# Turning the tail's first MLP layer around, and splitting the last output group

## The chip, the core and the metric

The kernel runs on one core of a Trainium2 chip. The metric is the time of one execution on the device in microseconds (us); the median of several runs is given. The profile is of one further execution, whose span from the first to the last instruction is 275.7 us.

## The reference

The computation is a linear attention followed by a gated MLP that mixes along the sequence.

```python
def phi(x):                               # x: (8, 8, 576, 64), w_phi: (64, 128)
    proj = np.einsum('bhsd,df->bhsf', x, w_phi)
    proj = proj - np.max(np.abs(proj), axis=-1, keepdims=True)
    return np.concatenate([np.exp(proj), np.exp(-proj)], axis=-1)
kv  = einsum('bhsf,bhsd->bhfd', phi(k), v);  z = phi(k).sum(2)
x   = einsum('bhsf,bhfd->bhsd', phi(q), kv) / (phi(q) @ z + 1e-6)   # -> (8, 576, 512)
h   = np.maximum(x @ w_in, 0)             # w_in: (512, 1024)
u, v = h[..., :512], h[..., 512:]
v_n = (v - mean(v)) / np.sqrt(var(v) + 1e-6)          # over the 512 features
v_s = einsum('ts,bsd->btd', w_spatial, v_n) + b_spatial[None, :, None]
out = (u * v_s) @ w_out                   # w_out: (512, 512)
```

The two halves u and v of the first MLP layer are what the change is about: v is normalized over its features and mixed over the tokens, u is multiplied with the result.

## The kernel before, in words

A batch has 576 tokens: four groups of 128 ("main") and 64 left over (the "tail", `TL = 64`). The tails of two successive batches share a tile, batch 2g in partitions 0 to 63 and batch 2g+1 in partitions 64 to 127; `bl` says which, and `r` is the slice of partitions or columns that belongs to it.

The attention (functions `a_...`) runs in units of a pair of heads, one after the other; in step i the stages of several units are interleaved by the list `ORDER`. When a batch's attention is done, `b_tasks(b)` puts the batch's MLP work in a queue, as (cost, function). After each stage of a step, `fill` takes tasks off the queue at a rate that spreads the queue's total cost over the steps that are left until the next batch's tasks come; the cost is an estimate of TensorE time, `MM` for four 512-column matmuls. So the matmuls of the MLP lie between those of the attention. What is left after the last step is issued in the queue's order. Within this the framework's scheduler may still order independent instructions of an engine differently.

The MLP of a batch, in the queue's order: an output group of the batch before; `b_v_tail` (the tail's v); two main groups of v (`b_v`); another output group; the other two of v; the roots and the tail's normalization (`b_root_tail`, `b_ln_tail`, `b_root`); normalization of the main v (`b_ln`) between output groups of the batch before and the four groups of u (`b_u`); `b_u_tail`; the mixing `b_s` and `b_s_tail`. The output of batch b waits for the queue of batch b + 1; that of the last batch stands at the end, the four main groups `b_o` and then `b_o_tail`.

Main v (`v_mm`, L447 to L451): for each 128 tokens, four matmuls with the tokens (xT) stationary and 512 columns of w_in moving, so the result has tokens in partitions; ACT applies the relu to a tile `vr` (L449); DVE takes mean and variance with bn_stats (L450) and bn_aggr (L451). `moments` (L455, L456) and `root` (on POOL, L461, L462) make scale and shift, and `normalize` (L467) writes `vn`, or `vnt` for the tail, on POOL and in the last batch on DVE. `b_v_tail` uses the same `v_mm` with the tail's 64 columns of `xTt` stationary.

Main u (`b_u`, L515, L517): w_in is stationary and the 512 tokens move, so the result has features in partitions, as `b_s` needs it. `b_u_tail` (L527, L529) does so for the 64 tokens of a tail: sixteen matmuls of 64 columns.

`b_s` (L536, L537, L539) needs all four `vn` tiles of its batch and `vnt`; DVE multiplies its result into `uT`. `b_s_tail` is L548 to L554. `o_mm` (L561, L564) makes an output group: four matmuls of 512 columns, a copy that alternates between DVE and ACT to a tile `ob`, and a transfer issued on SP's queue (L570 main, L576 tail, one for each batch of the pair).

[...] `vr` has five buffers, `ob` six, `uTt` one.

Of the kernel before, what the change touches and what calls it, by code (L numbers as in the profile page):

```python
# [8 lines left out]
FP32 = mybir.dt.float32  # L9
BF16 = mybir.dt.bfloat16  # L10
AF = mybir.ActivationFunctionType
# [5 lines left out]
def kernel(  # L17
# [15 lines left out]
    nc = tc.nc  # L33

    B, H, S, D = q.shape
    F = w_phi.shape[1]
    DM = moe_w_in.shape[0]
    DFF = moe_w_in.shape[1]
    HALF = DFF // 2
    P = 128  # L40
    KC = DM // P
    NP = H // 2
    NB = 4
    T0 = NB * P
    TL = S - T0
    G = B // 2
    POS = [0, 2, 1, 3]
    DA = D + 2

    cpool = ctx.enter_context(tc.tile_pool(name="const", bufs=1))  # L50
# [4 lines left out]
    s2 = ctx.enter_context(tc.tile_pool(name="stage_b", bufs=2))  # L55

    psum = ctx.enter_context(tc.tile_pool(name="psum", bufs=8, space=bass.MemoryType.PSUM))
# [13 lines left out]
    st = {}  # L71
    gs = {}
# [47 lines left out]
        pin(nc.sync.dma_start_transpose)(out=u[x + "T"], in_=src.rearrange("p h x -> p (h x)"))  # L120


    wphi_f = cpool.tile([P, F], FP32)
    for i in range(2):
        pin(nc.scalar.dma_start)(out=wphi_f[i * D:(i + 1) * D, :], in_=w_phi)
    alloc(0)
# [12 lines left out]
    bias = cpool.tile([P, NB], FP32)  # L139
# [4 lines left out]
    ident = cpool.tile([P, P], BF16)  # L144
# [40 lines left out]
    for y in range(2):  # L185
        r = slice(y * D, (y + 1) * D)
# [7 lines left out]
    for i in range(2):  # L194
        pin(nc.scalar.copy)(out=alternate(wm, i),
                            in_=wphi2[:, i * F:(i + 1) * F].unsqueeze(1).to_broadcast([P, NP, F]))
# [19 lines left out]
    w_in_bf = cpool.tile([P, KC, DFF], BF16)  # L216
    w_out_bf = cpool.tile([P, KC, DM], BF16)
# [226 lines left out]
    def v_mm(lhs, dst, r, stats, mv):  # L444
        pv = psum.tile([P, HALF], FP32, tag="bank", name="pv")
        for kc in range(KC):
            nc.tensor.matmul(out=pv[r], lhsT=lhs(kc), rhs=w_in_bf[:, kc, HALF:DFF],  # L447
                             start=(kc == 0), stop=(kc == KC - 1))
        nc.scalar.activation(out=dst[r], in_=pv[r], func=AF.Relu, bias=0.0, scale=1.0)  # L449
        nc.vector.bn_stats(out=stats[r], in_=dst[r])  # L450
        nc.vector.bn_aggr(out=mv[r], in_=stats[r])  # L451

    def moments(mv, r, n):
        m = small.tile([P, NB, 2], FP32, tag="var", name="var")
        nc.vector.tensor_scalar(out=m[r, 0:n, 0:1], in0=mv[r, 0:n, 1:2], scalar1=1e-6, scalar2=None, op0=ALU.add)  # L455
        nc.vector.tensor_scalar(out=m[r, 0:n, 1:2], in0=mv[r, 0:n, 0:1], scalar1=-1.0, scalar2=None, op0=ALU.mult)  # L456
        return m
# [11 lines left out]
    def b_v(b, j):  # L469
        d = st[b]  # L470
        if j == 0:
            d["vn"] = s2.tile([P, NB, HALF], BF16, tag="vn", name="vn", bufs=2)
            d["mv"] = small.tile([P, NB, 2], FP32, tag="mv", name="mv")
            d["vr"] = {}
        d["vr"][j] = s2.tile([P, HALF], BF16, tag="vr", name="vr", bufs=5)
        stats = small.tile([P, 6], FP32, tag="stats", name="stats")
        v_mm(lambda kc: d["xT"][:, kc, j * P:(j + 1) * P], d["vr"][j], slice(0, P), stats, d["mv"][:, j, :])
        if j == NB - 1:
            d["var"] = moments(d["mv"], slice(0, P), NB)

    def b_root(b):
        st[b]["rs"] = root(st[b]["var"], slice(0, P), NB)

    def b_ln(b, j):
        d = st[b]
        normalize(b, d["vn"][:, j, :], d["vr"][j], d["rs"][:, j, :])

    def b_v_tail(g, bls):
        d = gs[g]
        r = slice(bls[0] * TL, (bls[-1] + 1) * TL)  # L490
        vr = s2.tile([P, HALF], BF16, tag="vr", name="vr", bufs=5)
        stats = small.tile([P, 6], FP32, tag="stats", name="stats")
        mv = small.tile([P, 1, 2], FP32, tag="mv_t", name="mv_t")
        v_mm(lambda kc: d["xTt"][:, kc, r], vr, r, stats, mv[:, 0, :])
        d["ln"] = vr, moments(mv, r, 1)

    def b_root_tail(g, bls):
        d = gs[g]
        r = slice(bls[0] * TL, (bls[-1] + 1) * TL)
        d["rs"] = root(d["ln"][1], r, 1)  # L500

    def b_ln_tail(g, bls):
        d = gs[g]
        vr = d["ln"][0]
        for bl in bls:
            r = slice(bl * TL, (bl + 1) * TL)
            normalize(2 * g + bl, vnt[g % 2][r, bl, :], vr[r], d["rs"][r, 0, :])

    def b_u(b, dc):
        d = st[b]  # L510
        if dc == 0:
            d["uT"] = s2.tile([P, KC, T0], BF16, tag="uT", name="uT", bufs=1)
        pu = psum.tile([P, T0], FP32, tag="bank", name="pu")
        for kc in range(KC):
            nc.tensor.matmul(out=pu, lhsT=w_in_bf[:, kc, dc * P:(dc + 1) * P], rhs=d["xT"][:, kc, :],  # L515
                             start=(kc == 0), stop=(kc == KC - 1))
        nc.scalar.activation(out=d["uT"][:, dc, :], in_=pu, func=AF.Relu, bias=0.0, scale=1.0)  # L517

    def b_u_tail(g, bls):
        d = gs[g]  # L520
        if bls[0] == 0:
            d["uTt"] = s2.tile([P, KC, P], BF16, tag="uTt", name="uTt", bufs=1)
        r = slice(bls[0] * TL, (bls[-1] + 1) * TL)
        pu = psum.tile([P, KC, P], FP32, tag="bank", name="pu")
        for dc in range(KC):
            for kc in range(KC):
                nc.tensor.matmul(out=pu[:, dc, r], lhsT=w_in_bf[:, kc, dc * P:(dc + 1) * P],  # L527
                                 rhs=d["xTt"][:, kc, r], start=(kc == 0), stop=(kc == KC - 1))
        nc.scalar.activation(out=d["uTt"][:, :, r], in_=pu[:, :, r], func=AF.Relu, bias=0.0, scale=1.0)  # L529

    def b_s(b, dc):
        d = st[b]
        ps = psum.tile([P, T0], FP32, tag="bank", name="ps")
        cs = slice(dc * P, (dc + 1) * P)
        for sp in range(NB):
            nc.tensor.matmul(out=ps, lhsT=d["vn"][:, sp, cs], rhs=w_spT[:, sp, 0:T0], start=(sp == 0), stop=False)  # L536
        nc.tensor.matmul(out=ps, lhsT=vnt[b // 2 % 2][:, b % 2, cs], rhs=w_spT[:, NB + b % 2, 0:T0],  # L537
                         start=False, stop=True)
        nc.vector.tensor_tensor(out=d["uT"][:, dc, :], in0=ps, in1=d["uT"][:, dc, :], op=ALU.mult)  # L539
# [18 lines left out]
    def o_mm(lhs, r):  # L558
        po = psum.tile([P, DM], FP32, tag="bank", name="po")
        for dc in range(KC):  # L560
            nc.tensor.matmul(out=po[r], lhsT=lhs(dc), rhs=w_out_bf[:, dc, :], start=(dc == 0), stop=(dc == KC - 1))  # L561
        ob = s2.tile([P, DM], FP32, tag="ob", name="ob", bufs=6)
        turn[0] ^= 1
        (nc.vector.tensor_copy if turn[0] else nc.scalar.copy)(out=ob[r], in_=po[r])  # L564
        return ob

    def b_o(b, j):
        ob = o_mm(lambda dc: st[b]["uT"][:, dc, j * P:(j + 1) * P], slice(0, P))
        dst = bass.AP(tensor=out.tensor, offset=out.offset + b * S * DM + POS[j] * DM, ap=[[NB * DM, P], [1, DM]])
        nc.sync.dma_start(out=dst, in_=ob)  # L570

    def b_o_tail(g, bls):
        r = slice(bls[0] * TL, (bls[-1] + 1) * TL)
        ob = o_mm(lambda dc: gs[g]["uTt"][:, dc, r], r)
        for bl in bls:
            nc.sync.dma_start(out=out[2 * g + bl, T0:S, :], in_=ob[bl * TL:(bl + 1) * TL, :])  # L576
# [18 lines left out]
    MM = KC * T0 / 2400.0  # L595
    MS = (KC + 1) * T0 / 2400.0

    def out_tasks(b):
        ts = [(MM, lambda j=j: b_o(b, j)) for j in range(NB)]
        if b % 2:  # L600
            ts.append((MM, lambda: b_o_tail(b // 2, [0, 1])))
        return ts

    def b_tasks(b):

        g, bl = b // 2, b % 2
        outs = out_tasks(b - 1) if b else []
        vs = [(MM, lambda j=j: b_v(b, j)) for j in range(NB)]
        us = [(MM, lambda dc=dc: b_u(b, dc)) for dc in range(KC)]
        ss = [(MS, lambda dc=dc: b_s(b, dc)) for dc in range(KC)]  # L610
        ns = [(0.0, lambda j=j: b_ln(b, j)) for j in range(NB)]
        ts = outs[:1] + [(MM, lambda: b_v_tail(g, [bl]))] + vs[:2] + outs[1:2] + vs[2:]
        ts += [(0.0, lambda: b_root_tail(g, [bl])), (0.0, lambda: b_ln_tail(g, [bl])), (0.0, lambda: b_root(b))]
        if b == 0:
            ts += [(0.3, lambda i=i: transpose_spatial(i)) for i in range(NB + 2)]
        for y in range(NB):
            ts += ns[y:y + 1] + outs[2 + y:3 + y] + us[y:y + 1]
        ts += [(MM / 2, lambda: b_u_tail(g, [bl]))] + ss
        ts.append((MS / 2, lambda: b_s_tail(g, [bl])))
        return ts + (out_tasks(b) if b == B - 1 else [])  # L620

# [147 lines left out]
```

## Time and profile before

| | |
|---|---|
| time, median of 3 runs | 279.08 us (278.86 to 280.59) |
| profiled span | 275.7 us, TensorE clock 1.00 throughout |
| TensorE (PE) busy | 254.7 us, 92% |
| VectorE (DVE) busy | 236.5 us, 86% |
| ScalarE (ACT) busy | 218.1 us, 79% |
| GpSimd (POOL) busy | 184.4 us, 67% |
| chain that ended last | PE 70%, ACT 14%, DVE 11%, issue 3% |

PE is the matmul stream and PEld the weight loads that run beside it. "Busy" adds up the time in which an engine has an instruction in it; matmuls are pipelined, so a 512-column matmul lasts 379 ns while the next starts 216 ns later. In the groups' rows, the number after x is how often the group ran; then come its busy time and the mean of one in ns, then the idle time of the engine just before it and what ended that. In the waits, the three numbers are the total in us, the count and the longest. In the chain, a row is the start, the time by which the piece moved the end on, and what it was. In the timeline, a row is the start, the time taken, engine, line and operation, and in brackets the idle time before.

### The profile page before, as it was taken

To read this page: it belongs to the slowest core of one execution; us is meant where nothing else is said; L and a number is where in the kernel's file an instruction comes from. 1 tells how busy PE (TensorE), PEld (TensorE's weight loads), DVE (VectorE), ACT (ScalarE), POOL (GpSimd) and SP (SyncE) were. 2 spreads that over 40 slices of the span, in tenths; PEclk is the share of its full clock that TensorE was granted. 3 is DMA by queue.
4 is the path that set the end of the run, shared out by engine and by line. 5 is a ranking of instruction groups with operands and counts; after the bars stand their busy time and mean duration, and the time that the engine had idled before them with its cause. 6 is when DMAs were issued, how large, how long until landed. Compare 5 with 4: busy or idle time off the path is not lost.

```text
span 275.7 us, 8138 instructions
## 1 busy us (share of the span) xinstructions
PE 254.7 (92%) x3007; PEld 171.3 (62%) x3047; DVE 236.5 (86%) x614; ACT 218.1 (79%) x501; POOL 184.4 (67%) x312
## 2 busy tenths in 40 slices
PE   3778999999999999999998999999998999999993
PEld 2467776777665766666665775766655765554441
DVE  7989999879999889998889899988898897565751
ACT  7898999797698978999798979998798977633511
POOL 7999899999569945897787954997347632410200
PEclk9999999999999999999999999999999999999999
DMA  7999999999999997999999998899744301211115
GB/s 209 230 228 146 164 155 113 181 208 122 202 200 219 232 212 133 232 176 199 156 110 221 258 183 146 171 233 176 104 89 118 88 2 73 81 40 40 76 40 190
DMA packets 84840, 42.43 MB, mean 154 GB/s; under 512 B 51840, under 2 KB 80192, under 8 KB 84800
## 3 DMA queue, kind: packets, MB, share of 16 engines
q1 hardware_dynamic: 60240, 30.95, 54.5%
q0 software_dynamic: 24400, 10.89, 38.5%
q8 instruction: 24, 0.39, 0.6%
q14 instruction: 16, 0.13, 0.2%
q10 hardware_dynamic: 160, 0.07, 0.1%
HBM read 32.85 MB, written 9.44 MB: 153 GB/s over the span
## 4 chain that ended last, share of the span: by engine, by line
PE 70%; ACT 14%; DVE 11%; issue 3%; ACTq 0%; DVEq 0%
PE pv L447 10%; PE ps L536 10%; PE po L561 9%; PE pu L515 8%; PE ps L266 7%; ACT kf L281 7%; PE pv L378 4%; PE pn L398 4%; ACT qf L365 4%; DVE mk L278 3%; PE pq L344 3%; PE ps L537 2%; PE pn L426 2%; ACT vr L449 1%; PE pu L527 1%
## 5 line engine op out<-in xcount | busy, mean ns | idle before, releaser
L306 POOL TENSOR_TENSOR vs<-v_f,em 128x512 bf16<-128x512 f32 x64 | 65.4, 1042 | 27.8 <-ACT em L301 25.3
L281 ACT ACTIVATE kf<-ps 128x512 bf16<-128x512 f32 x144 | 75.4, 638 | 6.5 <-DVE mk L278 6.5
L365 ACT ACTIVATE qf<-pq 128x512 bf16<-128x512 f32 x128 | 66.6, 625 | 9.6 <-PE pq L344 7.5
L278 DVE TENSOR_REDUCE mk<-ps 128x4 f32<-128x512 f32 x72 | 46.3, 681 | 0.7
L292 DVE TENSOR_REDUCE mq<-ps 128x4 f32<-128x512 f32 x62 | 39.9, 678 | 2.2 <-PE ps L266 2.0
L561 PE MATMUL po<-w_out_bf,uT 128*128 128x512 bf16 x120 | 31.9, 379 | 1.4 <-ACT kf L281 0.8
L461 POOL TENSOR_TENSOR rs<-var,neghalf 64x1 f32<-64x1 f32 (+1 forms) x16 | 12.8, 797 | 30.5 <-DVE var L456 30.3
L536 PE MATMUL ps<-w_spT,vn 128*128 128x512 bf16 x119 | 32.5, 379 | 0.5
L450 DVE BATCH_NORM_STATS2 stats<-vr 128x6 f32<-128x512 bf16 (+1 forms) x40 | 26.7, 684 | 6.5 <-ACT vr L449 6.2
L447 PE MATMUL pv<-w_in_bf,xT 128*128 128x512 bf16 x117 | 30.7, 379 | 1.2 <-ACT kf L281 0.6
L515 PE MATMUL pu<-xT,w_in_bf 128*128 128x512 bf16 x119 | 31.1, 379 | 0.5 <-issue 0.2
L449 ACT ACTIVATE vr<-pv 128x512 bf16<-128x512 f32 (+1 forms) x40 | 23.8, 620 | 8.9 <-PE pv L447 8.1
L539 DVE TENSOR_TENSOR uT<-ps,uT 128x512 bf16<-128x512 f32 x32 | 22.0, 687 | 8.5 <-PE ps L537 7.6
L378 PE MATMUL pv<-vs,kf 128*128 128x66 bf16 x512 | 24.5, 193 | 1.3 <-ACT kf L281 1.1
L389 DVE TENSOR_TENSOR x<-pn,rc 128x256 bf16<-128x256 f32 x64 | 25.0, 416 | 0.3
L398 PEld LDWEIGHTS <-qf 128*128 128x128 bf16 x512 | 20.2, 97 | 7.4 <-issue 1.7
L517 ACT ACTIVATE uT<-pu 128x512 bf16<-128x512 f32 x32 | 19.7, 643 | 6.3 <-PE pu L515 3.2
L378 PEld LDWEIGHTS <-kf 128*128 128x128 bf16 x512 | 21.7, 97 | 3.6 <-issue 2.9
L398 PE MATMUL pn<-kv,qf 128*128 128x66 bf16 x512 | 21.9, 193 | 0.9 <-ACT kf L281 0.3
L380 PE MATMUL pv<-vst,kf 128*128 128x66 bf16 x128 | 21.2, 192 | 1.4 <-POOL vst L61 1.4
L564 ACT COPY ob<-po 128x512 f32<-128x512 f32 x18 | 11.0, 613 | 14.3 <-PE po L561 8.8
L467 POOL TENSOR_SCALAR vn<-vr,rs 128x512 bf16<-128x512 bf16 x28 | 21.2, 764 | 0.9
(130 smaller groups left out, 562.6 us busy)
## 6 DMA issues: line engine op xcount, KB each, us to landing
out_dram<-ob SPq DMA_DIRECT2D x32, 256.0 KB, 2.7
v_f<-in_v_dram SPq DMA_DIRECT2D x14, 512.0 KB, 5.6
k_bf<-in_k_dram POOLq DMA_DIRECT2D x14, 256.0 KB, 6.3
q_bf<-in_q_dram POOLq DMA_DIRECT2D x14, 256.0 KB, 5.9
qt<-qT_b SPq DMA_DIRECT2D x24, 64.0 KB, 4.2
v_tl<-in_v_dram SPq DMA_DIRECT2D x8, 128.0 KB, 5.9
v_f<-in_v_dram SPq DMA_DIRECT2D x1, 1024.0 KB, 8.8
w_in_bf<-in_moe_w_in_dram POOLq DMA_DIRECT2D x2, 512.0 KB, 7.0
```

Source lines behind the costliest of these rows:

```text
L278: nc.vector.tensor_reduce(out=u["mk"][:, hs], in_=pk, axis=AX.X, op=ALU.max, apply_absolute_value=True)
L281: nc.scalar.activation(out=u["kf"][:, s, hs, :], in_=pk, func=AF.Exp, bias=0.0, scale=sc)
L292: nc.vector.tensor_reduce(out=mq[:, 4 * half:4 * half + 4], in_=pq, axis=AX.X, op=ALU.max, apply_absolute_value=True)
L306: nc.gpsimd.tensor_tensor(out=vs[:, s, :, 0:D], in0=st[u["b"]]["v"][:, pj * H:(pj + 1) * H, :], in1=em[:, s, :].unsqueeze(2).to_broadcast( ...
L365: nc.scalar.activation(out=qf[:, s], in_=pq, func=AF.Exp, bias=0.0, scale=sc)
L378: nc.tensor.matmul(out=pv[:, hh, s, :], lhsT=u["kf"][:, s, 4 * hh + c, :], rhs=u["vs"][:, s, 4 * hh + c, :], start=(c == 0), stop=False)
L398: nc.tensor.matmul(out=pn[:, pos, :], lhsT=u["qf"][hh][:, s, pos, :], rhs=d["kv"][:, 2 * u["pj"] + hh, s, :], start=(s == 0), stop=(s == 1))
L447: nc.tensor.matmul(out=pv[r], lhsT=lhs(kc), rhs=w_in_bf[:, kc, HALF:DFF], start=(kc == 0), stop=(kc == KC - 1))
L450: nc.vector.bn_stats(out=stats[r], in_=dst[r])
L515: nc.tensor.matmul(out=pu, lhsT=w_in_bf[:, kc, dc * P:(dc + 1) * P], rhs=d["xT"][:, kc, :], start=(kc == 0), stop=(kc == KC - 1))
L536: nc.tensor.matmul(out=ps, lhsT=d["vn"][:, sp, cs], rhs=w_spT[:, sp, 0:T0], start=(sp == 0), stop=False)
L561: nc.tensor.matmul(out=po[r], lhsT=lhs(dc), rhs=w_out_bf[:, dc, :], start=(dc == 0), stop=(dc == KC - 1))
```

## The change

The tail's first MLP layer is done for u and v at once with w_in stationary: 32 matmuls of 64 moving columns into one PSUM bank, and two relus to `uTt` and `vTt`, both with features in partitions. v is needed with tokens in partitions, so a new task `b_turn_tail`, placed after the first two main groups of v, turns `vTt` back by four transposes on TensorE; DVE copies the result to `vr` and takes its statistics. `b_u_tail` goes away. `vTt` takes a buffer of `vr`'s ring, and `uTt` gets a second buffer, as it's now written earlier; the room comes from `wphi_f`, which moves from the constants to the ring of `ob`.

In the last batch the output order becomes: first main group, tail, the two middle groups, last main group. This last one (`b_o_last`) is made in two halves of 256 columns, each with its own PSUM bank; the first is copied by ACT and sent on ACT's queue, the second copied by DVE and sent on SP's. It is for shortening the time after the last matmul.

```diff
-    wphi_f = cpool.tile([P, F], FP32)
+    wphi_f = s2.tile([P, F], FP32, tag="ob", name="wphi_f", bufs=6)
...
     def b_v_tail(g, bls):
         d = gs[g]
+        if bls[0] == 0:
+            d["uTt"] = s2.tile([P, KC, P], BF16, tag="uTt", name="uTt", bufs=2)
+        d["vTt"] = s2.tile([P, KC, TL], BF16, tag="vr", name="vTt", bufs=5)
         r = slice(bls[0] * TL, (bls[-1] + 1) * TL)
+        pu = psum.tile([P, 2 * KC, TL], FP32, tag="bank", name="pu")
+        for dc in range(2 * KC):
+            for kc in range(KC):
+                nc.tensor.matmul(out=pu[:, dc, :], lhsT=w_in_bf[:, kc, dc * P:(dc + 1) * P],
+                                 rhs=d["xTt"][:, kc, r], start=(kc == 0), stop=(kc == KC - 1))
+        nc.scalar.activation(out=d["vTt"], in_=pu[:, KC:2 * KC, :], func=AF.Relu, bias=0.0, scale=1.0)
+        nc.scalar.activation(out=d["uTt"][:, :, r], in_=pu[:, 0:KC, :], func=AF.Relu, bias=0.0, scale=1.0)
+
+    def b_turn_tail(g, bls):
+        d = gs[g]
+        r = slice(bls[0] * TL, (bls[-1] + 1) * TL)
+        pt = psum.tile([P, KC, P], BF16, tag="bank", name="pt")
+        for dc in range(KC):
+            nc.tensor.transpose(out=pt[r, dc, :], in_=d["vTt"][:, dc, :], identity=ident)
         vr = s2.tile([P, HALF], BF16, tag="vr", name="vr", bufs=5)
...
-        v_mm(lambda kc: d["xTt"][:, kc, r], vr, r, stats, mv[:, 0, :])
+        nc.vector.tensor_copy(out=vr[r], in_=pt[r].rearrange("p n e -> p (n e)"))
+        nc.vector.bn_stats(out=stats[r], in_=vr[r])
+        nc.vector.bn_aggr(out=mv[r, 0, :], in_=stats[r])
         d["ln"] = vr, moments(mv, r, 1)
...
-    def b_u_tail(g, bls):
...
+    def b_o_last(b, j):
+        dst = bass.AP(tensor=out.tensor, offset=out.offset + b * S * DM + POS[j] * DM, ap=[[NB * DM, P], [1, DM]])
+        for y, copy, queue_ in ((0, nc.scalar.copy, nc.scalar), (1, nc.vector.tensor_copy, nc.sync)):
+            n = slice(y * DM // 2, (y + 1) * DM // 2)
+            po = psum.tile([P, DM // 2], FP32, tag="bank", name="po")
+            for dc in range(KC):
+                nc.tensor.matmul(out=po, lhsT=st[b]["uT"][:, dc, j * P:(j + 1) * P], rhs=w_out_bf[:, dc, n],
+                                 start=(dc == 0), stop=(dc == KC - 1))
+            ob = s2.tile([P, DM], FP32, tag="ob", name="ob", bufs=6)
+            copy(out=ob[:, 0:DM // 2], in_=po)
+            queue_.dma_start(out=dst[:, n], in_=ob[:, 0:DM // 2])
...
+        if b == B - 1:
+            ts = ts[:1] + ts[-1:] + ts[1:NB - 1] + [(MM, lambda: b_o_last(b, NB - 1))]
...
-        ts = outs[:1] + [(MM, lambda: b_v_tail(g, [bl]))] + vs[:2] + outs[1:2] + vs[2:]
+        ts = outs[:1] + [(MM, lambda: b_v_tail(g, [bl]))] + vs[:2]
+        ts += [(MM / 4, lambda: b_turn_tail(g, [bl]))] + outs[1:2] + vs[2:]
...
-        ts += [(MM / 2, lambda: b_u_tail(g, [bl]))] + ss
+        ts += ss
```

More of the change, by code (lines that the diff above doesn't have):

```diff
@@ L517, in b_u @@
         nc.scalar.activation(out=d["uT"][:, dc, :], in_=pu, func=AF.Relu, bias=0.0, scale=1.0)
-    def b_u_tail(g, bls):
[L520 to L529, printed above, removed]
     def b_s(b, dc):
```

## The prediction

> **What bounds the kernel now.** I read the page's first part (busy time of each engine), then the table of stretches, then the chain that ended last in order of time.
>
> ```profile
> PE 254.7 (92%) x3007; PEld 171.3 (62%) x3047; DVE 236.5 (86%) x614; ACT 218.1 (79%) x501; POOL 184.4 (67%) x312
> ```
> ```profile
> 100.00:140.00 40.00, 39.58 (x474) 26.74 (x480) 37.09 (x92) 35.64 (x84) 29.14 (x52) 1.00 1.07 175
> 140.00:180.00 40.00, 38.84 (x475) 26.36 (x480) 37.54 (x99) 35.73 (x85) 29.50 (x50) 1.00 1.18 186
> ```
>
> The columns of the stretches are the length, then PE, weight loads, DVE, ACT and POOL. PE is busy 39.6 of 40 us, and a busy PE need not be a full one; the chain is the better witness, where each entry's length is what it advanced the end:
>
> ```profile
> 110.63 1.03 PE pv L447 x4
> ...
> 126.79 0.47 PE pu L527 x16
> ```
> ```profile
> 244.28 0.22 PE pt L412 x4
> ```
>
> Elsewhere in that chain four 512-column matmuls advance PE by 0.86 us (0.216 each), sixteen 64-column ones (L527) by 0.47 (0.029 each) and four transposes by 0.22 (0.055 each). Between about 40 and 271 us the chain is mostly such runs: PE's issue rate sets the time. It leaves PE for ACT and DVE only around 76-91, 105-110, 145-150 and 199-210 us, at the start of a batch's MLP work. The waits of PE that these cost are short:
>
> ```profile
> PE pv L378 <- ACT kf L281: 1.1, 1, 1.1
> PE pt L259 <- ACT kf L281: 1.0, 1, 1.0
> ...
> PE po L561 <- ACT kf L281: 0.8, 1, 0.8
> ```
>
> DVE is second: 37.1 to 37.5 of 40 us, only 2.5 to 2.9 us free per 40.
>
> [...] a 128x512 bf16 copy out of PSUM takes 413 ns (L261), the fp32 one 678 (L564). [...] On SP's queue here, the last issues landed after 2.2 to 2.4 us.
>
> **The change part by part.** The rows I price it with:
>
> ```profile
> L449 ACT ACTIVATE vr<-pv 64x512 bf16<-64x512 f32 x8 | 4.7, 593 | 3.6 <-PE pv L447 3.6
> L529 ACT ACTIVATE uTt<-pu 128x256 bf16<-128x256 f32 x8 | 3.7, 469 | 0.0
> L261 DVE COPY qt<-pt 128x512 bf16<-128x512 bf16 x12 | 5.0, 413 | 0.3 <-PE pt L259 0.3
> ```
>
> *PE, per tail.* Removed: four matmuls of 512 columns, 0.86, and the sixteen of b_u_tail, 0.47; together 1.33 us. Added: 32 matmuls of 64 columns, 32 x 0.0294 = 0.94, and four transposes with 128 moving columns, 0.22; together 1.16. Net -0.17 us. There are eight tails. In the seven before the last batch PE sets the time, so 7 x -0.17 = **-1.2 us**.
>
> *ACT, per tail.* One 593 ns relu and one 469 ns relu become two of 469 ns: 1.06 to 0.94, -0.12 us in all. But they now both stand ahead of the batch's first b_v relus: 0.94 in place of 0.59 there, +0.35 us where the chain already visits ACT. The later u slot gives 0.47 back. I take zero, as PE's waits on ACT are few.
>
> *DVE, per tail.* One copy of a 64x512 bf16 bank, by L261 0.41 us (row length, not rows, sets it: the 64- and the 128-row bn_stats take 688 and 683). It replaces nothing, so 7 x 0.41 = 2.9 us lie on the second-busiest engine. Low end 0 (it fits in the free time), high end 2.9 (PE waits for all of it). I take **+0.3 us**: the waits list only short waits of PE on DVE after the start.
>
> *The new wait.* PE's transposes wait for the vTt relu. Two b_v groups (8 x 0.216 = 1.7 us of PE) stand between; the two relus need 0.94. Hidden unless ACT is over 1 us behind; behind the transposes on PE stand o1 and the later b_v groups. Buffers: vTt and vr together make six allocations per batch in a ring of five, but each reuses a tile of an earlier stage that has been read by then; two uTt tiles let the new u start before the previous group's output is done; w_phi in an ob slot is read in the first microseconds. All three cost nothing, and the queue's total cost, by which tasks are paced, falls by MM/4 of some 16 us per batch.
>
> *Last batch.* Here the tail's statistics lie on a DVE chain that ends in the vn tiles b_s needs:
>
> ```profile
> 255.17 0.70 DVE L450 BATCH_NORM_STATS2 stats<-vr 128x6 f32<-128x512 bf16 x1
> 255.78 0.68 DVE L564 COPY ob<-po 128x512 f32<-128x512 f32 x1
> 256.37 0.17 DVE L451 BATCH_NORM_AGGREGATE mv<-stats 128x2 f32<-128x6 f32 x1
> 256.58 0.42 DVE L467 TENSOR_SCALAR vnt<-vr,rs 64x512 bf16<-64x512 bf16 x1
> 257.03 0.69 DVE L450 BATCH_NORM_STATS2 stats<-vr 128x6 f32<-128x512 bf16 x1
> ...
> 261.98 0.40 DVE L467 TENSOR_SCALAR vn<-vr,rs 128x512 bf16<-128x512 bf16 x1
> ```
>
> From 255.2 to 259.0 DVE has no gap, then POOL's root (1.2 us), then vn. The last vn ends at 262.38, and PE's fourth b_s matmul starts at 262.45: it just waits. In the changed kernel the tail's statistics, now at 252.5 to 255.1 in idle time, move into this gapless stretch: copy, bn_stats, bn_aggr and two small ones, by start-to-start distances 0.33 + 0.60 + 0.20 + 0.24 = 1.4 us. Against that v1's bn_stats can start some 0.9 us sooner, as DVE stood ready for it. vn comes about 0.5 us later, while PE arrives 0.17 earlier: **+0.5 us**, with ends -0.17 (DVE's order hides it) and +1.0 (nothing is regained).
>
> *The end.*
>
> ```profile
> 270.36 0.69 DVE L564 COPY ob<-po 128x512 f32<-128x512 f32 x1 [1.03 <-PE po L561]
> ...
> 271.27 0.58 ACT L564 COPY ob<-po 128x512 f32<-128x512 f32 x1 [1.14 <-PE po L561]
> 271.88 1.11 SPq L576 DMA_DIRECT2D out_dram<-ob  x2
> ```
>
> The last PE work is the tail's output; ACT copies it (0.58), SP issues two transfers one after the other, the second at 272.40, landing at 274.78. The span ends 0.9 later. After the change PE still has twenty 512-column equivalents to do and ends at the same point. The last half is copied by DVE, 128x256 from PSUM in fp32: about 0.42 (by L389's 416 ns for that size). So the last SP issue comes near 271.72, not 272.40: -0.7. The other half leaves on ACT's queue about 0.4 earlier; the only transfers seen there, w_phi at the start, took 3.2 us to land for 32 KB. With that it lands near 274.5 (-0.3); with SP's 2.3 it isn't last. I take **-0.6**, ends -0.2 and -0.7. The tail's output, now second, needs uTt at 267.41, when o0 still runs: nothing.
>
> Sum: -1.2 + 0.3 + 0.5 - 0.6 = -1.0, so 279.08 - 1.0 = **278.1 us**.
>
> **Rivals.**
> (A) Evacuation pays part back. Half of DVE's 2.9 shows on PE (+1.45), the last chain costs its high end (+1.0), the end brings only 0.2: -1.2 + 1.45 + 1.0 - 0.2 = +1.05, **280.1**. For it: DVE at 98% in the windows 100 to 120. Against: PE keeps issuing in those very windows.
> (B) DVE and ACT become the bound at the start of each batch: all 2.9 of DVE, and ACT's +0.35 in half the batches, 7 x 0.17 = 1.2: -1.2 + 2.9 + 1.2 + 1.0 - 0.2 = +3.7, **282.8**, slower than before. For it: the chain's four visits to ACT and DVE lie exactly where the work is added. Against: ACT's total falls, and the later part has less to do.
> (C) The new order removes waits: PE's waits on ACT for L378, L561, L447 and L266 add up to 1.1 + 0.8 + 0.6 + 0.5 = 3.0 us in the waits list; half go (-1.5), the last batch gains its 0.17 and the end 0.7: -1.2 - 1.5 - 0.17 - 0.7 = -3.6, **275.5**. For it: less ACT work late in a batch. Against: the new relus stand at those very places.
>
> **How the numbers follow.** Chances: the forecast 0.60, A 0.17, B 0.10, C 0.13. Forecast and A lie within 1% (276.3 to 281.9), B above and C below: faster 0.13, same 0.77, slower 0.10. The range, 276.0 to 281.0, takes in A and reaches toward C: the forecast's own unknowns run from -1.2 + 0 - 0.17 - 0.7 (277.0) to A and a little over.
>
> **What would show it.** Right: 256 matmuls of 64 columns in pu, sixteen still advancing PE by 0.47 us; 32 new transposes; ACT's busy time about 1 us down, DVE's about 3 us up, PE's waits on DVE unchanged; the last vn near 262 minus 1.2 plus 0.5; the last issue on SP some 0.7 us nearer the last matmul. Wrong: PE waiting on the vTt relu or on the vr copy in most batches; a 64-column matmul that takes over 0.04 us in a run of 32; the half on ACT's queue landing last; or a chain that stays on DVE after 110 us.

## The result, and the profile after

The changed kernel takes **283.09 us** (median; 282.17 to 283.45), the kernel before 278.97 beside it (278.55 to 280.59): a ratio of **1.0132, with an interval of 1.0085 to 1.0178**. It is slower by 1.3%, and the forecast of 278.1 and its range up to 281.0 are both missed. Ratios here and below leave out executions over 1.5% longer than the same kernel's fastest; only turn_twice has such ones, two of its four.

The page of the kernel after, busy time of each engine and shares of the chain that ended last:

```profile
PE 257.9 (92%) x3179; PEld 175.7 (62%) x3179; DVE 240.7 (86%) x623; ACT 217.0 (77%) x501; POOL 183.9 (65%) x312
...
PE 58%; DVE 22%; ACT 8%; issue 4%; POOL 3%; DMA 2%; SPq 1%; ACTq 0%; POOLq 0%; DVEq 0%
```

ACT has lost 1.1 us, DVE has gained 4.2. The chain has moved: PE from 70% to 58%, DVE from 11% to 22%. The table of stretches (length, then PE, weight loads, DVE, ACT, POOL, then the granted clock of TensorE) says where PE lost its issue:

```profile
100.00:140.00 40.00, 39.81 (x518) 27.32 (x517) 36.80 (x89) 33.84 (x80) 28.07 (x48) 1.00 1.02 168
140.00:180.00 40.00, 37.75 (x471) 25.55 (x468) 36.19 (x94) 33.74 (x80) 28.82 (x50) 1.00 1.09 177
```

In the first stretch PE is as full as before. In the second it is busy 37.75 us, before 38.84, and DVE too has less to do there: both wait. The waits that end on the keys' work, first the kernel before, then the kernel after:

```profile
ACT kf L281 <- DVE mk L278: 6.5, 13, 0.8
```
```profile
ACT kf L281 <- DVE mk L278: 10.8, 12, 2.4
...
PE pv L378 <- ACT kf L281: 3.1, 2, 1.6
...
PE po L568 <- ACT kf L281: 1.2, 1, 1.2
```

ACT's exponentials (L281) waited 6.5 us in all for DVE's maxima (L278) before, at most 0.8 at once; now 10.8 and 2.4. PE then waits for those exponentials: 1.1 at L378 before, now 3.1.

**Where in the program.** I cut each trace at the first matmul of each tail's first layer, so each column is one batch's piece, the last up to the last `b_s_tail`:

| batch | 0 | 1 | 2 | 3 | 4 | 5 | 6 | 7 | sum |
|---|---|---|---|---|---|---|---|---|---|
| before | 33.73 | 33.01 | 29.19 | 30.39 | 29.64 | 30.55 | 23.33 | 15.49 | 225.33 |
| after | 33.36 | 33.27 | 28.80 | 33.21 | 28.96 | 32.17 | 23.16 | 16.56 | 229.49 |

The sum is 4.16 longer, which is the size of the result (4.12 between the medians). Every even batch is shorter, by 0.2 to 0.7; every odd one is longer, by 0.3 to 2.8. Ahead of the first cut 40.91 and 42.70 us pass, but a kernel with the same order there took 42.09, so that part varies by itself.

Within the pieces PE's issue work fell by 1.4 us, an estimate: each of the eight tails has four matmuls of 512 columns and sixteen of 64 less, 32 of 64 and four transposes of 128 more, and the traces of before and after have starts 216 ns apart at 512 columns, 56 at 128 and 29 at 64 (medians). PE's waits of over 0.25 us rose from 5.3 to 10.1 and the small ones by 0.7. The figures of before are taken from the run end_only, which has the same order in these pieces; the trace of before lacks 40 matmul records.

One thing that sets odd batches apart is that their tail lies in partitions 64 to 127; whether it is what costs them time is tested under "The hold". DVE's timeline of the kernel after, first batch 2, then batch 3 (start, time taken; the distance of two starts is what to read):

```profile
114.35 0.41 DVE L511 COPY vr<-pt 64x512 bf16<-64x512 bf16 x1
114.68 0.68 DVE L450 BATCH_NORM_STATS2 stats<-vr 128x6 f32<-128x512 bf16 x1
115.28 0.67 DVE L512 BATCH_NORM_STATS2 stats<-vr 64x6 f32<-64x512 bf16 x1
115.87 0.16 DVE L451 BATCH_NORM_AGGREGATE mv<-stats 128x2 f32<-128x6 f32 x1
...
143.50 1.29 DVE L278 TENSOR_REDUCE mk<-ps 128x4 f32<-128x512 f32 x2
...
145.42 0.43 DVE L511 COPY vr<-pt 64x512 bf16<-64x512 bf16 x1
145.87 0.18 DVE L451 BATCH_NORM_AGGREGATE mv<-stats 128x2 f32<-128x6 f32 x1
146.09 0.69 DVE L292 TENSOR_REDUCE mq<-ps 128x4 f32<-128x512 f32 x1
146.81 0.69 DVE L512 BATCH_NORM_STATS2 stats<-vr 64x6 f32<-64x512 bf16 x1
147.53 0.69 DVE L292 TENSOR_REDUCE mq<-ps 128x4 f32<-128x512 f32 x1
148.26 0.18 DVE L513 BATCH_NORM_AGGREGATE mv_t<-stats 64x2 f32<-64x6 f32 x1
...
152.76 1.28 DVE L278 TENSOR_REDUCE mk<-ps 128x4 f32<-128x512 f32 x2
```

In batch 2 the next instruction starts 0.59 us after the bn_stats, before that has ended. In batch 3 the starts lie 0.72 apart, and the copy takes 0.45 of DVE's time (145.42 to 145.87) where it took 0.33 (114.35 to 114.68). From 145.42 to 148.26 each instruction starts 0.03 us after the one ahead has ended, from 114.35 to 115.87 each starts 0.08 before that end. So in batch 3 each change between rows 0 to 127 and rows 64 to 127 comes with about 0.12 us more to the next start (0.72 against 0.59 to 0.60, 0.45 against 0.33). The start at 146.09, behind an instruction in the same rows 0 to 127, is late as well (0.21 after that one's start, 0.08 in after_low below); what makes DVE wait is not shown beyond these numbers.

In the kernel before, the same statistics stood elsewhere. DVE's timeline of batch 3:

```profile
138.54 0.41 DVE L330 COPY qT_b<-pt 16x512 bf16<-16x512 bf16 x1 [0.91 <-PE pt L327]
138.98 0.69 DVE L450 BATCH_NORM_STATS2 stats<-vr 64x6 f32<-64x512 bf16 x1
...
140.11 0.69 DVE L278 TENSOR_REDUCE mk<-ps 128x4 f32<-128x512 f32 x1
140.83 0.15 DVE L455 TENSOR_SCALAR var<-mv_t 64x1 f32<-64x1 f32 x1
...
148.15 1.28 DVE L278 TENSOR_REDUCE mk<-ps 128x4 f32<-128x512 f32 x2
```

Only one copy lies between an idle 0.91 us and the bn_stats. The hold, as I call this delay from here on, shows here too (140.11 to 140.83 is 0.72), but few such pairs stand in the full part. From one pair of maxima (L278) to the next, where the tail's statistics now lie, 8.04 us pass before (140.11 to 148.15); after, from 143.50 to 152.76, 9.26.

### The profile page after: what moved, and what is told of

It is laid out like the page before. It is cut to its first block, busy times and chain, and to the rows that moved or that the text cites. A ratio compares the mean times of both kernels' runs of the same rounds, so it can differ in the third digit from the quotient of the medians.

```text
span 281.4 us, 8437 instructions
## 1 busy us (share of the span) xinstructions
PE 257.9 (92%) x3179; PEld 175.7 (62%) x3179; DVE 240.7 (86%) x623; ACT 217.0 (77%) x501; POOL 183.9 (65%) x312
## 4 chain that ended last, share of the span: by engine, by line
PE 58%; DVE 22%; ACT 8%; issue 4%; POOL 3%; DMA 2%; SPq 1%; ACTq 0%; POOLq 0%; DVEq 0%
PE ps L543 10%; PE pu L534 7%; PE po L568 7%; PE ps L266 6%; DVE mk L278 4%; DVE stats L450 4%; PE pv L378 4%; PE pv L447 4%; ACT kf L281 4%; PE pn L398 3%; PE ps L544 2%; PE pq L344 2%; PE pu L497 2%; DVE mq L292 2%; DVE x L389 2%
## 5 line engine op out<-in xcount | busy, mean ns | idle before, releaser
L281 ACT ACTIVATE kf<-ps 128x512 bf16<-128x512 f32 x144 | 75.0, 624 | 11.2 <-DVE mk L278 10.8
L278 DVE TENSOR_REDUCE mk<-ps 128x4 f32<-128x512 f32 x72 | 46.2, 680 | 1.2 <-PE ps L266 0.7
L543 PE MATMUL ps<-w_spT,vn 128*128 128x512 bf16 x128 | 33.3, 379 | 0.7 <-DVE vn L467 0.7
L534 PE MATMUL pu<-xT,w_in_bf 128*128 128x512 bf16 x128 | 32.1, 379 | 0.0
L447 PE MATMUL pv<-w_in_bf,xT 128*128 128x512 bf16 x128 | 31.5, 379 | 0.0
L450 DVE BATCH_NORM_STATS2 stats<-vr 128x6 f32<-128x512 bf16 x32 | 21.6, 682 | 7.8 <-ACT vr L449 7.7
L378 PE MATMUL pv<-vs,kf 128*128 128x66 bf16 x512 | 24.5, 193 | 3.8 <-ACT kf L281 3.1
L378 PEld LDWEIGHTS <-kf 128*128 128x128 bf16 x512 | 21.8, 97 | 7.0 <-issue 5.8
L449 ACT ACTIVATE vr<-pv 128x512 bf16<-128x512 f32 x32 | 19.7, 624 | 5.4 <-PE pv L447 4.9
L571 ACT COPY ob<-po 128x512 f32<-128x512 f32 x17 | 10.2, 600 | 15.0 <-PE po L568 15.0
```

The source lines that it names most:

```text
L278: nc.vector.tensor_reduce(out=u["mk"][:, hs], in_=pk, axis=AX.X, op=ALU.max, apply_absolute_value=True)
L281: nc.scalar.activation(out=u["kf"][:, s, hs, :], in_=pk, func=AF.Exp, bias=0.0, scale=sc)
L378: nc.tensor.matmul(out=pv[:, hh, s, :], lhsT=u["kf"][:, s, 4 * hh + c, :], rhs=u["vs"][:, s, 4 * hh + c, :], start=(c == 0), stop=False)
```

## The experiments

Three causes are to be told apart: the **copy** on DVE, the tail's **relus** both early on ACT, and the **place** of the tail's statistics, behind two main groups where DVE has no gap. A fourth, the **hold** of DVE instructions in partitions 64 to 127, enters with the last five runs; what the earlier ones seemed to say of place is read again after them. "Pieces" is the sum defined above, from one profile each; kernels with the same order on TensorE there repeat it to 0.1 us (before, end_only and ob_placed; after and mid_only). In four traces, those of turn_act, turn_twice, turn_late and stats_late_copy, TensorE's granted clock falls to half for 3.4 us once or twice within the pieces; in the others it doesn't. This is told with the runs.

| run | median us | ratio to before, interval | pieces |
|---|---|---|---|
| end_only | 278.58 | 1.0003 [0.9989, 1.0017] | 225.37 |
| mid_only | 283.74 | 1.0186 [1.0137, 1.0235] | 229.50 |
| turn_act | 280.14 | 1.0060 [1.0039, 1.0080] | 228.53 |
| turn_twice | 289.81 | 1.0330 [1.0248, 1.0411] | 235.8 |
| turn_late | 289.56 | 1.0391 [1.0354, 1.0428] | 236.6 |
| turn_early | 281.91 | 1.0121 [1.0090, 1.0151] | 228.96 |
| u_late | 282.19 | 1.0120 [1.0086, 1.0155] | 228.75 |
| before_copy | 279.23 | 1.0008 [0.9994, 1.0022] | 225.9 |
| stats_late | 282.79 | 1.0130 [1.0089, 1.0171] | 229.38 |
| stats_late_copy | 290.35 | 1.0402 [1.0364, 1.0441] | 236.6 |
| early_act | 280.63 | 1.0073 [1.0042, 1.0104] | 227.69 |
| ob_placed | 278.91 | 0.9996 [0.9974, 1.0018] | 225.42 |
| before_low | 277.31 | 0.9940 [0.9918, 0.9962] | 223.77 |
| stats_late_low | 279.60 | 1.0019 [1.0003, 1.0035] | 226.13 |
| after_low | 278.69 | 0.9999 [0.9982, 1.0017] | 225.50 |
| early_act_low | 279.96 | 1.0047 [1.0030, 1.0063] | 226.67 |
| after_high | 285.28 | 1.0242 [1.0216, 1.0269] | 231.80 |

### The two halves of the change

end_only is the kernel before with only the new end; mid_only is the changed kernel without it.

```diff
-        if b == B - 1:
-            ts = ts[:1] + ts[-1:] + ts[1:NB - 1] + [(MM, lambda: b_o_last(b, NB - 1))]
```

> The kernel before with only the last batch's output order and the split last group (its instructions are otherwise in the same order). Prediction's own term: -0.6 us. What the changed kernel's profile shows: -0.2 us from the last matmul to the end (4.3 instead of 4.5), since the half on ACT's queue takes 3.1 us to land. Theory 'loss is in the middle': 278.8, not measurably different. A theory in which the end costs the 4 us: about 283.

> The changed kernel with the outputs of the last batch as before: only the tail's first layer is changed. Theory 'loss is in the middle and in the last batch': as slow as the changed kernel or 0.2 us slower, about 283.3 (+4.3 over before). If the end were the cause: about 278.

The end is worth nothing that can be told; the loss is in the middle. The changed kernel's last rows, in the timeline of all engines:

```profile
277.18 0.42 DVE L588 COPY ob<-po 128x256 f32<-128x256 f32 x1 [0.18 <-PE po L585]
277.19 0.36 ACTq L589 DMA_DIRECT2D out_dram<-ob  x1
277.64 0.41 SPq L589 DMA_DIRECT2D out_dram<-ob  x1
```

And the last transfers, issued from 277.1 us on (size, us from issue to landing):

```profile
out_dram<-ob SPq DMA_DIRECT2D x1, 256.0 KB, 2.9
out_dram<-ob ACTq DMA_DIRECT2D x1, 128.0 KB, 3.1
out_dram<-ob SPq DMA_DIRECT2D x1, 128.0 KB, 2.8
```

SP issues 0.5 us after the last matmul (1.2 before), as hoped. But the half that it sends takes 2.8 us to land, where the last transfer of the kernel before took 2.4, and lands last, at 280.5; the half on ACT's queue takes 3.1 and lands 0.2 us ahead of it. So it is not ACT's queue alone, as the expectation of end_only has it: all three transfers issued within this half microsecond land late. Whether their overlap is the reason is not shown. From the last matmul to the end: 4.5 us before, 4.3 after.

### The copy

turn_act moves it to ACT, turn_twice does it twice, before_copy adds an unused one of the same time to the kernel before, from the tail's own PSUM bank (for room it also moves wphi_f to the ring of ob, as the change does).

```diff
 turn_act
-        nc.vector.tensor_copy(out=vr[r], in_=pt[r].rearrange("p n e -> p (n e)"))
+        nc.scalar.copy(out=vr[r], in_=pt[r].rearrange("p n e -> p (n e)"))
 turn_twice
+        nc.vector.tensor_copy(out=vr[r], in_=pt[r].rearrange("p n e -> p (n e)"))
 before_copy, in b_v_tail of the kernel before
+        nc.vector.tensor_copy(out=spare[r, 0:HALF // 2], in_=pv[r, 0:HALF // 2])
```

> The changed kernel with the copy of the turned v out of PSUM on ACT instead of DVE: TensorE's instructions keep their order. It takes 8 x 0.41 us off DVE and puts 8 x about 0.6 us on ACT. Theory D (DVE is the queue that is too long at the start of a batch, so that the maxima of the keys come late): 2 us or more faster than the changed kernel, 280 to 281. Rival R (the two relus standing early on ACT delay the exponentials): ACT gets still more there, so slower, 284 or more. Rival O (the new order and pacing of TensorE's work): order unchanged, so 283.

> The changed kernel with the DVE copy of the turned v made twice, so that its cost is doubled (the framework's order of the other instructions shifts somewhat as well). Theory D: another 2 to 3.3 us, 285 to 286.5. Rivals R and O: within 1 us of the changed kernel, in either direction.

> The kernel before plus one unused DVE copy of 64x256 fp32 out of the tail's v bank (about 0.42 us) per tail, so DVE's added cost without the turn, the new relus or the new statistics' place (the framework's order of the rest shifts as well). Theory D with the sum of DVE's work: 280.5 to 282. If only the place of the tail's statistics counts, or R: 279, as before.

turn_act has a median 2.95 us under the changed kernel's, and ACT pays for the copy; its groups by shape show

```profile
L511 ACT COPY vr<-pt 64x512 bf16<-64x512 bf16 x8 | 4.6, 576 | 0.1
```

Its profiled execution was one of its longest, and its pieces are only 1.0 shorter. The table of stretches shows why:

```profile
211.30:214.70 3.40, 1.77 (x39) 1.42 (x38) 3.34 (x8) 2.06 (x6) 2.44 (x5) 1.00 0.09 24
214.70:218.10 3.40, 3.40 (x14) 1.49 (x13) 1.18 (x5) 1.86 (x7) 3.40 (x5) 0.50 0.38 111
```

PE waits for half of 3.4 us, and in the next 3.4 us the granted clock is 0.50: PE is busy throughout, but with 14 matmuls. At half the clock these 3.4 us hold 1.7 us of full-speed work, so such a stretch can cost up to 1.7 us (an estimate from the 0.50 and the 3.4 us). The piece in which it lies, batch 5's, is 1.2 longer than the changed kernel's; the other seven together are 2.2 shorter, which fits the median better. turn_twice (at 95.2 and 221.5 us), turn_late (133.9 and 198.8) and stats_late_copy (154.3 and 219.2) have two such stretches each, every time after 3.4 us in which PE is busy for only 1.2 to 1.5. Not every wait is followed by one: after has none behind its emptiest 3.4 us (1.8 us busy, from 88.7).

A second copy costs 6.3 us in the pieces of turn_twice's trace, which is of one of its two longest executions. 4.4 of them lie in batches 1 and 5, where TensorE runs at half the clock; the other six pieces are 1.9 longer, so the 6.3 is no price of the copy's own 8 x 0.41 = 3.3 us. A copy in the old place costs 0.3 by the medians, which is within the interval, and 0.6 in the pieces. So the copy is dear only where it now stands.

### The place

turn_late puts the turn and the tail's normalization behind the second group of u, turn_early the turn behind the first group of v; early_act is turn_early with the copy on ACT. stats_late is the kernel **before** with nothing but its tail's bn_stats, bn_aggr and moments issued behind two groups of v; nothing is added.

```diff
 turn_early
-        ts = outs[:1] + [(MM, lambda: b_v_tail(g, [bl]))] + vs[:2]
-        ts += [(MM / 4, lambda: b_turn_tail(g, [bl]))] + outs[1:2] + vs[2:]
+        ts = outs[:1] + [(MM, lambda: b_v_tail(g, [bl]))] + vs[:1]
+        ts += [(MM / 4, lambda: b_turn_tail(g, [bl]))] + vs[1:2] + outs[1:2] + vs[2:]
 turn_late, after the group of u with y == 1
+                ts += [(MM / 4, lambda: b_turn_tail(g, [bl])), (0.0, lambda: b_root_tail(g, [bl])),
+                       (0.0, lambda: b_ln_tail(g, [bl]))]
 stats_late, in the kernel before
-        ts = outs[:1] + [(MM, lambda: b_v_tail(g, [bl]))] + vs[:2] + outs[1:2] + vs[2:]
+        ts = outs[:1] + [(MM, lambda: b_v_tail(g, [bl]))] + vs[:2]
+        ts += [(0.0, lambda: b_stats_tail(g, [bl]))] + outs[1:2] + vs[2:]
 stats_late_copy, ahead of stats_late's bn_stats, from the second main group's bank
+        nc.vector.tensor_copy(out=spare[r], in_=st[2 * g + bls[0]]["pv"][r, 0:HALF // 2])
```

> The changed kernel with the turn (transposes, copy, statistics, roots and normalization of the tail's v) moved from between the second and third group of v to after the second group of u, some 8 us later, where DVE has free time. The same instructions. Theory D (DVE's queue is too long at the start of a batch, so the keys' maxima of the unit that follows come late): most of the loss in the middle goes, 279.5 to 281, and the late maxima of units 15, 24 and 33 (3.5, 4.1 and 3.4 us after TensorE in the changed kernel, 2.5, 2.4 and 2.2 before) are back near those of before. Rival R (the early relus on ACT): 283. A third possibility is that the normalized tail comes too late for the mixing, which TensorE would then wait for: over 283.

> The changed kernel with the turn one group of v earlier. The same instructions. If what hurts is that the tail's statistics now stand late in DVE's burst: 1 to 2 us faster than the changed kernel, unless TensorE waits for the relu. If only the sum of DVE's work counts, or with rival R: 283.

> The changed kernel with the turn after the first main group of v and its copy on ACT: both cures together, TensorE's order that of the earlier turn. Theory P: 279 to 280, as the statistics are nearer their old place and DVE has no more work than before; what may remain is TensorE waiting for the relu. If it were the sum of TensorE's waits for the relu and nothing else: 282, as with the earlier turn alone.

> The kernel before, with nothing added: only bn_stats, bn_aggr and the two small operations of the tail are issued after the second main group of v, where the changed kernel has them, instead of right after the tail's own relu. Theory P (place: what hurts is that the tail's statistics leave an idle moment of DVE and go into the stretch in which it has no gap, ahead of the keys' maxima): 280 to 281.5. If the place doesn't matter: 278.9.

> As the kernel before with the late statistics, plus an unused DVE copy of 64x256 fp32 (about 0.42 us) from the second main group's v bank just ahead of them, so that DVE's work and order are those of the changed kernel while TensorE and ACT work as before. Theory P with the copy counting only in this place: 282 to 284. If the turn itself (TensorE and ACT) makes the loss: within 1 us of the kernel before.

turn_late, far over the 279.5 to 281 hoped for, has another wait, for the tail's normalized v (from its waits), and the two stretches at half the clock:

```profile
PEld L544 <- POOL vnt L467: 9.9, 5, 3.0
...
PE ps L544 <- POOL vnt L467: 7.5, 5, 2.5
```

turn_early brings DVE's maxima back near their old time. In one unit each of batches 1, 3 and 5 the first maximum starts 2.64, 2.61 and 2.68 us after the end of its matmuls; before 2.49, 2.41, 2.17; after 3.47, 4.10, 3.41. But the weight loads of the transposes then wait 1.9 us for the vTt relu, and PE 1.0 of it, and the run gains only about 1 us (0.5 in the pieces). early_act, which has the copy on ACT besides, took 280.63, over the 279 to 280 expected and no less than turn_act alone.

stats_late is the strongest of these: the move alone costs 3.9 us, more than the 280 to 281.5 expected, with PE's order unchanged. (It loses 0.6 to 1.1 us in each of the batches 1 to 5 and in 7, so not in odd ones alone, as the expectation of stats_late_low has it.) Its waits, as in the kernel after:

```profile
ACT kf L281 <- DVE mk L278: 8.7, 13, 2.0
...
PE pv L378 <- ACT kf L281: 1.7, 2, 1.6
```

DVE's timeline of its batch 3 has no copy in it, and the same hold (0.72 from L505 on):

```profile
147.40 0.69 DVE L505 BATCH_NORM_STATS2 stats<-vr 64x6 f32<-64x512 bf16 x1
148.12 0.18 DVE L451 BATCH_NORM_AGGREGATE mv<-stats 128x2 f32<-128x6 f32 x1
...
151.93 1.28 DVE L278 TENSOR_REDUCE mk<-ps 128x4 f32<-128x512 f32 x2
```

stats_late_copy lost 7.2 us more in the pieces, far over its 8 x 0.41. 4.4 of that lie in batches 3 and 5, which hold its stretches at half the clock. It also keeps a main group's bank until the late copy; how the rest divides is not settled.

### The relus, and relief for DVE

u_late does only v early and u in its old place. ob_placed is the kernel before with the output copies dealt by group, so that the one in the full stretch always goes to ACT.

```diff
 u_late
-        for dc in range(2 * KC):
+        for dc in range(KC, 2 * KC):
...
-        ts += ss
+        ts += [(MM / 2, lambda: b_u_tail(g, [bl]))] + ss
 ob_placed, in o_mm; b_o gives act = (j % 2 == 1)
-        (nc.vector.tensor_copy if turn[0] else nc.scalar.copy)(out=ob[r], in_=po[r])
+        (nc.scalar.copy if act else nc.vector.tensor_copy)(out=ob[r], in_=po[r])
```

> The changed kernel with only v done early; the tail's u has its own bank and relu at the old place before the mixing. It takes the second relu (0.47 us) off ACT and 16 matmuls off TensorE at the start of each batch. Rival R: 280 to 281. Theory D: 283, as DVE's work is unchanged.

> The kernel before with another DVE operation of the full stretch taken out: output group 1 of each list, which stands between the second and third main group of v, is always copied by ACT, and groups 0 and 2 by DVE (before, the alternation ran on over the batches, so three of seven batches had a 0.68 us copy by DVE there). TensorE's order is unchanged. Theory P: these three batches lose up to 0.68 us each of DVE's stretch, one of them the last, where it lies in the chain to the normalized v: 277.6 to 278.5. If DVE's stretch isn't what TensorE waits for: 278.9.

u_late lies 0.9 us under the changed kernel with overlapping intervals: the early relus of u are a small part at most. ob_placed brought the maxima of batch 3 from 2.41 to 1.90 us behind TensorE, and no time: ACT got what DVE gave up.

### The hold

Each of the next kernels works the tail's statistics, root and normalization in fixed rows; only the normalized result still goes to its own rows. "low" is rows 0 to 63 in every batch, "high" rows 64 to 127. Kinds and sizes of instructions are unchanged.

```diff
     def b_turn_tail(g, bls):
         d = gs[g]
-        r = slice(bls[0] * TL, (bls[-1] + 1) * TL)
+        r = slice(0, TL)
...
-        d["rs"] = root(d["ln"][1], r, 1)
+        d["rs"] = root(d["ln"][1], slice(0, TL), 1)
...
-            normalize(2 * g + bl, vnt[g % 2][r, bl, :], vr[r], d["rs"][r, 0, :])
+            normalize(2 * g + bl, vnt[g % 2][r, bl, :], vr[0:TL], d["rs"][0:TL, 0, :])
```

(after_high has TL to P for 0 to TL; before_low and stats_late_low write the tail's v into rows 0 to 63 by the matmul itself. So the rows of TensorE's output and of the root on POOL move as well; no run moves DVE's alone.)

> The kernel before, with the tail's v, statistics, root and normalization worked in partitions 0 to 63 in every batch (before: 64 to 127 in odd batches); only the normalized result is still written to its own rows. Same number of instructions and same sizes. Hold theory (a DVE instruction whose partitions start elsewhere than those of the one ahead waits until that one is done, about 0.12 us for each such change, seen in odd batches only): the changes of place become fewer, but lie here in a stretch where DVE has idle time, so 278.0 to 278.9. Place theory (only the queue's place of the statistics counts): 278.9, no change.

> The kernel before with only the tail's statistics issued later, after two main groups of v, as in the run of that name, and in partitions 0 to 63 in every batch. The same move in partitions 0 to 63 or 64 to 127 cost 3.9 us, lost in batches 1, 3, 5 and 7 alone. Hold theory: most of that goes, 279.0 to 280.5, DVE starts the statistics' neighbours 0.60 us apart and not 0.72, and the keys' maxima of units 24 and 33 lie under 3 us behind TensorE. Place theory: odd batches lose since their start falls into a fuller stretch of DVE, whatever the partitions: 282 to 283, lateness 3.2 to 3.6 us as before.

> The changed kernel with the turned tail, its copy, statistics, root and normalization in partitions 0 to 63 in every batch. Hold theory: about five to seven fewer waits of 0.12 us in the stretch of each odd batch, 0.6 to 0.9 us less lateness there, 279.5 to 281.0. Place theory: 282.5 to 283.5, as the changed kernel.

> The run of the turn after one main group with its copy on ACT (280.6), with the tail in partitions 0 to 63 in every batch. Hold theory: 278.5 to 280.0, a little less than 280.6 as less of the loss was left. Place theory: 280.6, no change.

> The changed kernel with the turned tail, its copy, statistics, root and normalization in partitions 64 to 127 in every batch: the opposite of the run in partitions 0 to 63, which won 0.8 to 1.1 us in each of the batches 1, 3, 5 and 7 and nothing in the even ones. Hold theory: the odd batches stay as in the changed kernel, the tail's instructions in batches 0, 2, 4 and 6 now start 0.72 us apart where they started 0.60 apart, and some of these batches lose up to 1 us each where DVE has no idle time to take it: 284 to 287. Theory that something else of odd batches is behind it: 283, no change.

| batch | 0 | 1 | 2 | 3 | 4 | 5 | 6 | 7 |
|---|---|---|---|---|---|---|---|---|
| before_low less before | 0.00 | -0.43 | +0.01 | -0.35 | -0.01 | -0.68 | 0.00 | -0.10 |
| stats_late_low less stats_late | +0.02 | -1.00 | +0.01 | -0.83 | +0.01 | -0.84 | 0.00 | -0.62 |
| after_low less after | 0.00 | -0.92 | 0.00 | -0.82 | -0.02 | -1.12 | 0.00 | -1.11 |
| after_high less after | +0.87 | 0.00 | +0.43 | 0.00 | +1.01 | -0.01 | +0.01 | 0.00 |

Only the batches whose rows were changed move, and of the even ones 0, 2 and 4 lose when they are put high. after_low, DVE's timeline of batch 3:

```profile
142.29 1.29 DVE L278 TENSOR_REDUCE mk<-ps 128x4 f32<-128x512 f32 x2
...
144.09 0.40 DVE L511 COPY vr<-pt 64x512 bf16<-64x512 bf16 x1
144.42 0.17 DVE L451 BATCH_NORM_AGGREGATE mv<-stats 128x2 f32<-128x6 f32 x1
144.50 0.65 DVE L292 TENSOR_REDUCE mq<-ps 128x4 f32<-128x512 f32 x1
145.08 0.68 DVE L512 BATCH_NORM_STATS2 stats<-vr 64x6 f32<-64x512 bf16 x1
145.68 0.67 DVE L292 TENSOR_REDUCE mq<-ps 128x4 f32<-128x512 f32 x1
...
150.73 1.27 DVE L278 TENSOR_REDUCE mk<-ps 128x4 f32<-128x512 f32 x2
```

The copy is back at 0.33 and the bn_stats at 0.60; from one pair of maxima to the next it is 8.44 us (142.29 to 150.73), after 9.26. after_high, batch 2, has 0.72 where the kernel after had 0.59:

```profile
115.30 0.69 DVE L512 BATCH_NORM_STATS2 stats<-vr 64x6 f32<-64x512 bf16 x1
116.02 0.18 DVE L451 BATCH_NORM_AGGREGATE mv<-stats 128x2 f32<-128x6 f32 x1
```

Counted over the traces from 40 us on, DVE instructions that start within 0.06 us after the end of the one ahead, with no overlap, are 98 before, 83 in before_low, 112 after, 78 in after_low and 140 in after_high.

before_low beats both kernels; it and after_low came in 0.7 and 0.8 us under what the hold let expect. early_act_low came in at the top of what the hold let expect: with the hold gone, the turn on ACT and one group earlier no longer pays, after_low being 1.3 us faster.

## Why the prediction was wrong

**What makes the 4.2 us.** In the pieces the holds cost the changed kernel 3.99 (after less after_low) and the kernel before 1.56 (before less before_low), so **2.4 us** of the loss is hold that the change added, 1.4 of it in the seven pieces before the last and 1.0 in the last. The other **1.7** (after_low less before_low) stays without any difference in rows: 3.1 of waits and small gaps against 1.4 of matmul work saved. The medians say the same, 2.7 and 1.4. In stats_late_low the place alone costs 2.4 over before_low, about 0.4 to 0.7 in each of the batches 2 to 5; so the place is enough to explain the remainder in size. But in after_low it falls in batches 3 and 5 alone (+2.35 and +1.18 over before_low, the others shorter or equal), so how it divides between place, copy and relus stays open. In batch 3 of after_low the maxima named above still start 3.30 us after their matmuls (2.26 in before_low). turn_act's 2.95 and after_low's 4.4 can't be added: with the copy on ACT its own held starts go too, and no run has only the copy on ACT with low rows.

**The step that failed** is the one on DVE, per tail: "by L261 0.41 us (row length, not rows, sets it ...). It replaces nothing", of which it takes "+0.3 us". The seven pieces before the last are 3.1 us longer though PE has 1.2 us less to issue: in place of the 0.3 stand 4.3 us of waits and gaps. 1.4 of them are hold, and 2.9 stay in after_low, as much as the high end that the prediction gave the term, but not shown to be the copy's. It went wrong in two ways. It priced only the new copy, and let the tail's statistics move into the full stretch of the seven batches for nothing; their move was counted for the last batch alone. And it priced by duration, when what DVE gives up is the distance to the next start, 0.60 us for a bn_stats of 0.69, which in rows 64 to 127 was 0.12 us more on either side (0.72). The waits then carry it on: maxima late, the exponentials behind them late (10.8 us waited for the maxima, 6.5 before), PE waiting for those (3.1 us at L378, 1.1 before). In the chain that is the sign named as wrong, a chain that stays on DVE after 110 us: from 113 to 122 us it lies on DVE alone but for gaps of 0.04 us at most.

**Point by point.**
- *PE:* -1.2 predicted for seven tails; -1.4 for all eight by the measured distances of two starts, which is the same per tail. Right: the chain has the pieces.

```profile
138.29 0.93 PE pu L497 x32
...
171.50 0.93 PE pu L497 x32
```

- *ACT:* busy time about 1 us less was forecast, 1.1 less measured, though the two relus take 0.41 us each where 0.47 was priced:

```profile
L500 ACT ACTIVATE uTt<-pu 128x256 bf16<-128x256 f32 x8 | 3.3, 414 | 0.0
...
L511 DVE COPY vr<-pt 64x512 bf16<-64x512 bf16 x8 | 3.3, 414 | 0.5 <-PE pt L507 0.4
```

- *DVE:* the copy is 0.41 us long, as priced, and waits for the transposes only 0.4 us in eight. Busy time rose by 4.2 instead of 3; in rows 0 to 63 it rises by just the 3 (235.0 in before_low, 238.0 in after_low).
- *The last batch:* +0.5 predicted with an upper end of +1.0; measured 16.56 - 15.49 = +1.07. after_low has 15.45 against 15.39 in before_low: all but 0.06 of the 1.07 is hold. So the work that the term had counted shows as 0.06 in place of 0.5, and what it had not counted makes the rest.
- *The end:* -0.6 predicted, -0.2 measured, its lower bound. The issue on SP came 0.7 us nearer the last matmul, as forecast, but the transfer took 2.8 us to land in place of 2.3; the half on ACT's queue took 3.1, near the 3.2 of w_phi, and did not land last.
- *Rivals:* B's 282.8 came nearest in size. Its account, 2.9 of copy plus ACT's relus, holds in part at most: turn_act's 2.95 looks like it, but a copy in the old place costs 0.3, u's relus 0.9 at most, and 2.4 of the loss goes with the rows.

Without the hold, after_low's 278.69 lies near the forecast of 278.1. But it stands against before_low's 277.31, 1.4 slower where 1.0 faster was forecast, so the agreement is chance.

## What to carry to other kernels

Price an operation on DVE by the distance to the next start (here 0.60 us for a bn_stats of 0.69), and look whether its rows begin where its neighbours' do: working the tail's statistics in rows 0 to 63 made the kernel before 0.6% faster with no instruction fewer. When a change moves a consumer later, count it as work added to the stretch where it lands, even when nothing is new: ask what stands behind it on that engine and who waits for that. Cut the trace at a landmark of each batch: comparing odd with even batches showed what sums over the span hide. Look at the granted clock of each stretch before a longer wait is priced: four traces here have TensorE at half the clock just behind one.

## What the runs showed of the hardware

- On DVE the start after the tail's 0.69 us bn_stats, among instructions in rows 0 to 127, came 0.59 to 0.60 us after its own with the tail in rows 0 to 63 (batch 2 of the changed kernel, batch 3 of after_low) and 0.72 with it in rows 64 to 127 (batch 3 of the changed kernel, batch 2 of after_high). After the tail's copy of 0.40 to 0.43 us it came after 0.33 and 0.45.
- TensorE's granted clock fell to 0.50 for 3.4 us in four traces, seven times within the pieces, each time after 3.4 us in which PE was busy for 1.2 to 1.8 us.
- At the end of the changed kernel a 128 KB store issued on ACT's queue landed in 3.1 us, and one issued on SP's 0.45 us later in 2.8; the last stores of the kernel before, on SP's queue, took 2.2 to 2.4.
